# Two late blocks of a causal convolution computed on VectorE in fp32 single taps, with weight copies of their own and new tables of ranks

## The chip, the cores and the metric

The kernel runs on one core of one Trainium2 chip. The metric is the device time of one execution in microseconds (us). TensorE (PE) does the matmuls, VectorE (DVE) and ScalarE (ACT) move and combine data, GpSimd (POOL) issues the loads of x and of the weights, and SyncE (SP) issues the transfers to and from DRAM that go through its queue. All of them work on the same 16 DMA engines.

## The reference

The input x is 8 batches of 3200 positions by 256 channels. A filter is applied along the positions in the frequency domain, and the result goes through a gated linear unit whose gate comes from a causal convolution with 5 taps per channel:

```python
def _attn_ref(x, filt_r, filt_i):
    X = np.fft.rfft(x, axis=1)
    F = (filt_r + 1j * filt_i)[None, :, :]
    y = np.fft.irfft(X * F, n=x.shape[1], axis=1)
    return y.astype(np.float32)

def _moe_ref(x, w_val, conv_w, w_out):
    B, S, D = x.shape
    K = conv_w.shape[0]                       # 5
    xp = np.concatenate([np.zeros((B, K - 1, D)), x], axis=1)
    gate_pre = np.zeros((B, S, D))
    for k in range(K):
        gate_pre += conv_w[k][None, None, :] * xp[:, k:k + S, :]
    gate = 1.0 / (1.0 + np.exp(-gate_pre))
    return (gate * (x @ w_val) @ w_out).astype(np.float32)

# reference: _moe_ref(_attn_ref(x, filt_r, filt_i), ...)
```

## The kernel before

**Stages of a batch.** The transform of length 3200 is split into 100 by 32. For each batch, in order:

- `load_x`: eight loads of x (200 KB each, cast to bf16), issued by POOL into ten buffers `xt`.
- `s1` (matmuls on L467): eight steps of two matmuls, the transform of length 100; `so` evicts each from PSUM into the tile so.
- `turn` (L486): four transposes on VectorE that bring the 32 residues onto partitions.
- `s2` (L496): seven groups, the transform of length 32; `xs` evicts, and `zed` (L512) multiplies with the filter on VectorE: the spectral product z.
- `inva` (L527): seven groups, the first half of the inverse (the inverse-A product); `ue` evicts into the tile u, of which there is one buffer.
- `wr` writes u to a DRAM scratch (escr) and `lv` reads it back in another layout (vt, one buffer), both on SP's queue. Only batch 0 turns u on VectorE instead (`back`, L568).
- `ib` (L578): eight steps, the second half of the inverse; `ye` (L587, ScalarE) evicts them into yt, which has four zero columns (`halo`, a memset on POOL) ahead of its 3200 positions.

Then come the gate and the value, in seven blocks of positions, six of 512 and one of 128 (a quarter block):

- `conv` (L609): 20 matmuls with 64 by 64 diagonal matrices dg_t, two halves of the channels by five taps, four of them in the array's four quarters at a time. Its output lies with the channels in an order of its own.
- `gate` (L619, ScalarE): the sigmoid, from PSUM into gt.
- `val` (L628): four matmuls with wv_t, whose columns are permuted as the convolution's channels are.
- `gv` (L643, VectorE): the product of val in PSUM and gt.
- `outp` (L651): eight matmuls of gv with wo_t, permuted likewise; `oe` evicts, and `store` writes to DRAM from one of five buffers o.

**Who does what.** The evictions so, xs, ue and oe can go to either ScalarE (L458) or VectorE (L460); the products, transposes and gv are VectorE's alone, the gates and ye ScalarE's alone. PSUM is four slots of two banks; each of the matmul steps takes one slot until its eviction frees it.

**What sets the order.** `Plan` lists every step with a cost for each engine that can do it, what it depends on and which buffers it takes and gives back. It walks through time, and on each free engine puts the ready step of the lowest rank. The rank of a step is eight times the batch number plus `LAG[stage]`, plus `FIRST[stage]` for batch 0, plus `STEP[stage]` times the step's number. `STAY` is added for a change of the TensorE mode (row-tiled steps s2, inva, conv against the others), `LEAN` for an eviction on VectorE. The list that comes out is the fixed order of instructions on every engine. An engine executes its list in order, so an instruction that waits holds back all that stand behind it on that engine.

**The weights.** POOL waits until the filter has arrived (`gate_loads`), issues ten loads of x, then the eight weight DMAs of `load_w`, then further loads of x as buffers come free.

Of the kernel before, what the change touches and what calls it, by code (L numbers as in the profile page):

```python
# [20 lines left out]
NV = 4 * NS  # L21
TURN = (0,)

LAG = dict(lx=-36, s1=-112.5, so=-60, t=188, pd=-44.5, s2=33.5, xs=111.5, z=-11, ia=44.5,
           ue=37.5, k=-47, ib=73, ye=38.5, cv=84, ga=-76.5, vl=75, gv=-70.5, op=82, oe=29)
FIRST = dict(lx=-69, s1=32.5, so=44.5, t=56.5, pd=-52, s2=8, xs=4.5, z=-13, ia=-16.5, ue=49.5,
             k=-34, ib=-10.5, ye=10.5, cv=10.5, vl=-27.5, gv=3, op=99.5, oe=-45.5)
CONV = 1.0
STEP = dict(lx=0.25, s1=0.8, so=1.4, t=0.8, s2=1.25, xs=0.4, z=2.35, ue=0.5, k=1.35, ib=0.15,
            ye=1.8, cv=0.1, ga=2.1, vl=0, gv=0.4, op=0.2, oe=0.2)  # L30
STAY, LEAN = 17.5, 12
RC = 4
NCH = R // RC
UCH = [(m, min(2, NM - m)) for m in range(0, NM, 2)]
BLK = 512
NB = 7
MAGIC = 12582912.0
SEM = dict(PE=0.2, ACT=0.13, DVE=0.13, none=0.0)


class Plan:
# [9 lines left out]
    def add(self, name, engines, rank, deps, emit, take=(), give=(), land=0.0, mode=None,  # L51
            ps=0, free=()):
        self.tasks[name] = dict(engines=engines, rank=rank, deps=deps, emit=emit, take=take,
                                give=give, land=land, mode=mode, ps=ps, free=free, slots=[])

    def places(self, n):
        if n == 0:
# [7 lines left out]
    def run(self):  # L65
        left = dict(self.tasks)
        users, need = {}, {}
        for n, t in left.items():
            need[n] = len(t["deps"])
            for d in t["deps"]:  # L70
                users.setdefault(d, []).append(n)
        ready_at = {n: 0.0 for n in left}
        free = {}
        mode = turn = None
        gives = []
        ready = {n for n in left if need[n] == 0}
        order = []
        now = 0.0
        while left:
            gives.sort(key=lambda v: v[0])  # L80
            while gives and gives[0][0] <= now + 1e-9:
                for pool in gives.pop(0)[1]:
                    if isinstance(pool, int):
                        self.slots.append(pool)
                    else:
                        self.room[pool] += 1
            best = None
            for n in ready:
                t = left[n]
                if ready_at[n] > now + 1e-9:  # L90
                    continue
                if self.places(t["ps"]) is None or any(self.room[p] < 1 for p in t["take"]):
                    continue
                for e, cost in t["engines"].items():
                    if free.get(e, 0.0) <= now + 1e-9:
                        away = e == "PE" and t["mode"] != mode
                        other = e == "DVE" and len(t["engines"]) > 1
                        key = (t["rank"] + (self.stay if away else 0.0)
                               + (self.lean if other else 0.0), cost)
                        if e == "DQ":  # L100
                            key = (ready_at[n] + (1e4 if t["mode"] == turn else 0.0), 0.0)
# [36 lines left out]
        return order  # L138
# [3 lines left out]
def kernel(  # L142
# [37 lines left out]
    dg_t = cpool.tile([128, 2, K, 64], BF16, name="dg_t")  # L180
    wv_t = cpool.tile([128, 2, D], BF16, name="wv_t")
    wo_t = cpool.tile([128, 2, D], BF16, name="wo_t")

    dpool = ctx.enter_context(tc.tile_pool(name="scr", bufs=2, space=bass.MemoryType.DRAM))
    pp = ctx.enter_context(tc.tile_pool(name="ps", bufs=1, space=bass.MemoryType.PSUM))
    ps_all = pp.tile([128, 4, 1024], FP32, name="ps")
    NXT = 10
    xpool = ctx.enter_context(tc.tile_pool(name="xin", bufs=NXT))
    sopool = ctx.enter_context(tc.tile_pool(name="s1o", bufs=1))
    tpool = ctx.enter_context(tc.tile_pool(name="s2i", bufs=1))  # L190
# [81 lines left out]
    def load_w():  # L272
        for dh in range(2):
            for r in range(2):
                ch = 128 * dh + 64 * r
                nc.gpsimd.dma_start(
                    out=wv_t[:, dh, :].rearrange("p (r h j) -> p h r j", r=2, h=2)[:, r],
                    in_=moe_w_val[128 * dh:128 * dh + 128, 128 * r:128 * r + 128]
                    .rearrange("p (h j) -> p h j", h=2))
                nc.gpsimd.dma_start(out=wo_t[64 * dh:64 * dh + 64, r, :],  # L280
                                    in_=moe_w_out[ch:ch + 64, :])

    def sp_setup():
        cw = g["cw"] = g1.tile([128, 2, K], FP32, name="cw")
# [9 lines left out]
                                      in_=f_t[p:p + 32, w, :, m0:m1, :])  # L294

    def cf_dve():
        idx = g1.tile([128, 2, 2, 32], FP32, name="idx")
        V.scalar_tensor_tensor(idx[...], g["k1f"][...], g["pcol"][:, 0:1], g["phf"][...],
                               op0=ALU.mult, op1=ALU.add)
        ts(idx[...], idx[...], 0.01, ALU.mult)  # L300
# [146 lines left out]
        hold = g1.tile([128, 1], BF16, name="hold")  # L447
        nc.gpsimd.tensor_copy(hold[...], f_t[:, 1, 1, NM - 1, 0:1])

    NGB, NOB = 3, 5  # L450
    vpool = ctx.enter_context(tc.tile_pool(name="ivi", bufs=1))
    ypool = ctx.enter_context(tc.tile_pool(name="yout", bufs=2))
    gpool = ctx.enter_context(tc.tile_pool(name="gate", bufs=NGB))
    opool = ctx.enter_context(tc.tile_pool(name="ost", bufs=NOB))

    def copy(e, dst, src, **kw):
# [145 lines left out]
    def conv(b, c):  # L602
# [9 lines left out]
                                 start=(k == 0), stop=(k == K - 1))  # L612
        st["cv", b, c] = ps

    def gate(b, c):
        ps = st.pop(("cv", b, c))
        g = gpool.tile([128, 2, BLK], BF16, name="gt")
        w = width(c)
        nc.scalar.activation(g[:, :, 0:w], two_banks(ps, w), AF.Sigmoid)  # L619
        st["G", b, c] = g  # L620

    def val(b, c):
# [3 lines left out]
        for eh in range(2):  # L626
            for dh in range(2):
                nc.tensor.matmul(ps[:, 512 * eh:512 * eh + w],  # L628
                                 lhsT=wv_t[:, dh, 128 * eh:128 * eh + 128],
                                 rhs=y[:, dh, H + BLK * c:H + BLK * c + w],  # L630
                                 start=(dh == 0), stop=(dh == 1))
        st["vl", b, c] = ps
# [13 lines left out]
    def outp(b, c):  # L646
        gv_ = st.pop(("GV", b, c))
        ps = psum()
        for a in range(width(c) // 128):
            for eh in range(2):  # L650
                nc.tensor.matmul(ps[:, D * a:D * a + D],  # L651
                                 lhsT=gv_[:, eh, 128 * a:128 * a + 128], rhs=wo_t[:, eh, :],
                                 start=(eh == 0), stop=(eh == 1))
        st["op", b, c] = ps

# [7 lines left out]
    def store(b, c):  # L663
# [4 lines left out]
            in_=o[:, 0:w // 128 * D])  # L668


    plan = Plan(dict(xt=NXT, so=1, t=1, xs=3, z=3, u=1, e=2, v=1, y=2, g=NGB, gv=NGB, o=NOB), 4,
                stay=STAY, lean=LEAN)
    add = plan.add

# [7 lines left out]
    for b in range(B):  # L682
# [65 lines left out]
        add(f"ha{b}", {"POOL": 0.2}, at("ib"), [f"ye{b},0"], lambda e, b=b: halo(b))  # L748
        for c in range(NB):
            f = width(c) / BLK  # L750
            add(f"cv{b},{c}", {"PE": 1.08 * f}, at("cv", c),
                [f"ye{b},{j}" for j in range(NCH)] + [f"ha{b}", "dg0", "dg1"],
                lambda e, b=b, c=c: conv(b, c), ps=1, take=("g",), mode=1)
            add(f"ga{b},{c}", {"ACT": 0.77 * f + 0.16}, at("ga", c), [f"cv{b},{c}"],
                lambda e, b=b, c=c: gate(b, c), free=[f"cv{b},{c}"])
            add(f"vl{b},{c}", {"PE": 0.87 * f}, at("vl", c),
                [f"cv{b},{c}"] + ([f"vl{b},{c - 1}"] if c else []), lambda e, b=b, c=c: val(b, c),
                ps=1, take=("gv",), give=("y",) if c == NB - 1 else (), mode=0)
# [78 lines left out]
```

## Time and profile before

| | |
|---|---|
| time, median of 3 runs | 308.13 us (307.31 to 309.5) |
| the profiled execution | 308.17 us, of which 306.3 us are its span |
| mean granted TensorE clock | 0.975 of full speed |
| busy, share of the span: TensorE | 263.4 us (86%) |
| VectorE | 255.6 us (83%) |
| ScalarE | 254.3 us (83%) |
| GpSimd | 58.0 us (19%) |
| DMA: SP's queue, share of 16 engines | 50.4%, 51.79 MB |
| DMA: GpSimd's queue | 30.6%, 15.08 MB |
| chain that ended last, by engine | TensorE 41%, VectorE 20%, DMA 14%, ScalarE 12% |

The profile is one execution. Its span runs from the first to the last recorded instruction; the rest of the execution's time lies around it. A busy TensorE is not TensorE at its peak, because matmuls are pipelined. The idle time of an engine matters where that engine is the one that the others wait for, so the shares have to be read by stretches of the span, not as an average over it.

### The profile page before, as it was taken

The numbers are of one execution on the slowest core, as the hardware profiler recorded it, in microseconds if no ns is written. First come the engines' busy times: TensorE is split into PE (matmuls) and PEld (weight loads), VectorE is DVE, ScalarE is ACT, GpSimd is POOL, SyncE is SP. The second block draws the span as 40 slices with busy tenths as digits, with TensorE's granted clock in tenths as the row PEclk, the third lists the DMA queues.
The fourth block names the chain that finished last, engine by engine and source line by source line (L and its number), as shares of the span: only waits on it lengthen the run. The fifth ranks groups of instructions, "written<-read, shape, count | busy, mean of one in ns | idle before, by whom it ended". The sixth has DMA issues, their size and how long they took to land.

```text
span 306.3 us, 8876 instructions
## 1 busy us (share of the span) xinstructions
PE 263.4 (86%) x3658; PEld 160.3 (52%) x3684; DVE 255.6 (83%) x284; ACT 254.3 (83%) x301; POOL 58.0 (19%) x120
## 2 busy tenths in 40 slices
PE   2831789889988898999699999998999999999993
PEld 0120526345446446754467447836577676566562
DVE  7688997889999899998399999989999985455442
ACT  3864879999799899997689999999889977786663
POOL 8584467520140050032000210000000000000000
PEclk9999955999999999999999999999999999999998
DMA  6999599998899989999599898858355993947255
GB/s 91 185 161 164 95 183 122 187 189 219 282 218 274 344 161 246 299 268 230 156 286 324 263 218 269 317 204 280 121 190 210 327 333 108 327 162 277 89 208 223
DMA packets 53208, 67.44 MB, mean 220 GB/s; under 512 B 7792, under 2 KB 34032, under 8 KB 53168
## 3 DMA queue, kind: packets, MB, share of 16 engines
q1 hardware_dynamic: 41264, 51.79, 50.4%
q0 software_dynamic: 11904, 15.08, 30.6%
q8 instruction: 29, 0.48, 0.6%
q14 instruction: 11, 0.09, 0.1%
HBM read 42.08 MB, written 38.14 MB: 262 GB/s over the span
## 4 chain that ended last, share of the span: by engine, by line
PE 41%; DVE 20%; DMA 14%; ACT 12%; issue 6%; POOL 4%; SPq 0%; DVEq 0%; ACTq 0%; POOLq 0%
PE ps L609 12%; PE ps L651 10%; PE ps L628 9%; DVE xs L460 6%; DVE z L512 6%; DMA xt<-in_x_dram 5%; PE ps L578 4%; DVE gv L643 4%; DMA escr<-u 4%; ACT yt L587 3%; PE ps L527 3%; ACT so L458 3%; DVE u L460 3%; DMA f_t<-in_filt_r_dram 2%; PE ps L467 2%
## 5 line engine op out<-in xcount | busy, mean ns | idle before, releaser
L643 DVE TENSOR_TENSOR gv<-ps,gt 128x1024 bf16<-128x1024 f32 (+1 forms) x56 | 60.7, 1100 | 24.4 <-PE ps L628 17.5
L512 DVE TENSOR_TENSOR z<-xs,f_t 128x2048 bf16<-128x2048 bf16 (+1 forms) x56 | 62.1, 1140 | 1.5 <-DMA f_t<-in_filt_i_dram 0.9
L609 PE MATMUL ps<-yt,dg_t 64*64 64x512 bf16 (+1 forms) x1120 | 60.7, 354 | 0.6 <-ACT yt L587 0.5
L458 ACT ACTIVATE so<-ps 128x1024 bf16<-128x1024 f32 x55 | 53.7, 1044 | 7.9 <-PE ps L467 5.6
L619 ACT ACTIVATE gt<-ps 128x1024 bf16<-128x1024 f32 (+1 forms) x56 | 52.0, 944 | 7.7 <-PE ps L609 5.4
L587 ACT ACTIVATE yt<-ps 128x800 bf16<-128x800 f32 x64 | 51.4, 852 | 7.0 <-PE ps L578 6.8
L467 PE MATMUL ps<-xt,cf_t 100*128 100x512 bf16 x128 | 45.5, 443 | 11.2 <-DMA xt<-in_x_dram 7.1
L202 POOL DMA_DIRECT2D xt<-in_x_dram x64 | 35.4, 557 | 100.5 <-PE ps L467 96.5
L651 PE MATMUL ps<-wo_t,gv 128*128 128x256 bf16 x400 | 51.8, 272 | 0.6 <-DVE gv L643 0.6
L628 PE MATMUL ps<-yt,wv_t 128*128 128x512 bf16 (+1 forms) x198 | 50.5, 354 | 1.8 <-DVE xs L460 0.3
L458 ACT ACTIVATE o<-ps 128x1024 f32<-128x1024 f32 (+1 forms) x41 | 38.9, 957 | 10.0 <-PE ps L651 9.2
L609 PEld LDWEIGHTS <-dg_t 64*64 64x64 bf16 x1120 | 31.1, 106 | 21.8 <-issue 3.0
L651 PEld LDWEIGHTS <-gv 128*128 128x128 bf16 x400 | 37.0, 97 | 8.7 <-DVE gv L643 1.3
L458 ACT ACTIVATE u<-ps 128x1024 bf16<-128x1024 f32 (+1 forms) x35 | 35.4, 1022 | 7.2 <-PE ps L527 5.4
L486 DVE STREAM_TRANSPOSE tt<-so 128x1024 f32<-128x1024 f32 x32 | 38.4, 1225 | 2.6 <-ACT so L458 2.6
L527 PE MATMUL ps<-z,a_t 64*64 64x256 bf16 x416 | 28.3, 288 | 13.1 <-DVE z L512 9.0
L578 PEld LDWEIGHTS <-vt 104*128 104x128 bf16 (+1 forms) x512 | 30.1, 102 | 9.1 <-issue 2.4
L578 PE MATMUL ps<-ci_t,vt 104*128 104x100 f16 (+1 forms) x512 | 33.9, 214 | 0.7 <-DVE gv L643 0.4
L496 PE MATMUL ps<-tt,w_t 64*64 64x256 bf16 x416 | 23.2, 291 | 9.7 <-DVE tt L486 5.6
L460 DVE CAST xs<-ps 128x1024 bf16<-128x1024 f32 (+1 forms) x27 | 30.7, 1156 | 0.5 <-PE ps L496 0.4
L458 ACT ACTIVATE xs<-ps 128x1024 bf16<-128x1024 f32 (+1 forms) x29 | 27.2, 974 | 4.1 <-PE ps L496 4.1
L628 PEld LDWEIGHTS <-wv_t 128*128 128x128 bf16 x224 | 18.7, 97 | 19.8 <-issue 5.6
(94 smaller groups left out, 192.3 us busy)
## 6 DMA issues: line engine op xcount, KB each, us to landing
out_dram<-o SPq DMA_DIRECT2D x48, 512.0 KB
xt<-in_x_dram POOLq DMA_DIRECT2D x64, 200.0 KB, 7.2
escr<-u SPq DMA_DIRECT2D x42, 256.0 KB
vt<-escr SPq DMA_DIRECT2D x56, 192.0 KB
out_dram<-o SPq DMA_DIRECT2D x8, 128.0 KB
f_t<-f_t SPq DMA_DIRECT2D x4, 224.0 KB
escr<-u SPq DMA_DIRECT2D x7, 128.0 KB
vt<-escr SPq DMA_DIRECT2D x56, 16.0 KB
```

Source lines behind the costliest of these rows:

```text
L458: nc.scalar.activation(dst, src, AF.Copy, **kw)
L460: nc.vector.tensor_copy(dst, src)
L467: nc.tensor.matmul(ps[:, 512 * h:512 * h + 512], lhsT=cf_t[0:L].rearrange("p h c i -> p (h c i)"), rhs=xv[:, DQ // 2 * h:DQ // 2 * h + DQ ...
L486: nc.vector.transpose(dst, src)
L512: nc.vector.tensor_tensor(z[:, :, :, 0:nm * D], st.pop(("XS", b, u))[:, :, 0:nm * D].unsqueeze(1) .to_broadcast((128, 2, 2, nm * D)), f_t[ ...
L578: nc.tensor.matmul(ps[:, o:o + L], lhsT=v[rows, RC * j + a, 128 * dh:128 * dh + 128], rhs=ci_t[rows, way, :], start=True, stop=True)
L587: nc.scalar.activation(y[:, :, H:H + N].rearrange("p h (a r) -> p h a r", r=R)[:, :, :, RC * j:RC * j + RC], ps[:, :].rearrange("p (h n) - ...
L609: nc.tensor.matmul(ps[64 * dh:64 * dh + 64, 512 * r:512 * r + w], lhsT=dg_t[rows, dh, k, :], rhs=y[rows, dh, BLK * c + k:BLK * c + k + w], ...
L619: nc.scalar.activation(g[:, :, 0:w], two_banks(ps, w), AF.Sigmoid)
L628: nc.tensor.matmul(ps[:, 512 * eh:512 * eh + w], lhsT=wv_t[:, dh, 128 * eh:128 * eh + 128], rhs=y[:, dh, H + BLK * c:H + BLK * c + w], sta ...
L643: nc.vector.tensor_tensor(o, i0, i1, op=ALU.mult)
L651: nc.tensor.matmul(ps[:, D * a:D * a + D], lhsT=gv_[:, eh, 128 * a:128 * a + 128], rhs=wo_t[:, eh, :], start=(eh == 0), stop=(eh == 1))
```

## The change

The convolution of block 5 of batch 6 and of block 3 of batch 7 no longer runs on TensorE. `side` computes it on VectorE: for each of the two channel halves a tensor_scalar with tap 0 and four scalar_tensor_tensor with taps 1 to 4, each of 128 partitions by 512 elements, from yt (bf16) into a tile acc (fp32, one buffer), ten instructions per block. The sigmoid of such a block reads acc from SBUF in place of PSUM. Since acc has the channels in their natural order, val and outp of these blocks use unpermuted copies of the weights, wvs_t and wos_t, loaded by two more DMAs at the end of `load_w`.

There are nine buffers xt for ten and four buffers o for five, and the table's index tile idx shares the memory of phf. All values of LAG, FIRST, STEP, STAY and LEAN are new, so the order of the instructions changes on every engine, and with it the engine of many evictions. Ranks are compared after rounding, and ties go by the order in which the steps were added.

```diff
-LAG = dict(lx=-36, s1=-112.5, so=-60, t=188, pd=-44.5, s2=33.5, xs=111.5, z=-11, ia=44.5,
-           ue=37.5, k=-47, ib=73, ye=38.5, cv=84, ga=-76.5, vl=75, gv=-70.5, op=82, oe=29)
...
+LAG = dict(lx=-102, s1=-149.5, so=-28, t=-14.5, pd=22, s2=-148, xs=31, z=101.5, ia=35.5,
+           ue=174.5, k=-68.5, ib=48.5, ye=-127, cv=77, ga=-150, vl=-28, gv=-180, op=58, oe=-187)
...
-STAY, LEAN = 17.5, 12
+STAY, LEAN = 47.5, 70.5
...
+SIDE = [(6, 5), (7, 3)]
+SIDERANK = 0
...
-                        key = (t["rank"] + (self.stay if away else 0.0)
-                               + (self.lean if other else 0.0), cost)
+                        key = (round(t["rank"] + (self.stay if away else 0.0)
+                                     + (self.lean if other else 0.0), 6), cost, t["at"])
...
+    wvs_t = cpool.tile([128, 2, D], BF16, name="wvs_t")
+    wos_t = cpool.tile([128, 2, D], BF16, name="wos_t")
...
-    NXT = 10
+    NXT = 9
...
+        nc.gpsimd.dma_start(out=wvs_t[...], in_=moe_w_val.rearrange("(h p) e -> p h e", h=2))
+        nc.gpsimd.dma_start(out=wos_t[...], in_=moe_w_out.rearrange("(h p) e -> p h e", h=2))
...
-        idx = g1.tile([128, 2, 2, 32], FP32, name="idx")
+        idx = g["phf"]
...
-    NGB, NOB = 3, 5
+    NGB, NOB = 3, 4
...
+    apool = ctx.enter_context(tc.tile_pool(name="acc", bufs=1))
...
+    def side(b, c, n):
+
+        k, dh = n // 2, n % 2
+        if n == 0:
+            st["A", b, c] = apool.tile([128, 2, BLK], FP32, name="acc")
+        w = width(c)
+        acc = st["A", b, c][:, dh, 0:w]
+        src = st["Y", b][:, dh, BLK * c + k:BLK * c + k + w]
+        cw = g["cw"][:, dh, k:k + 1]
+        if k == 0:
+            nc.vector.tensor_scalar(acc, src, cw, None, op0=ALU.mult)
+        else:
+            nc.vector.scalar_tensor_tensor(acc, src, cw, acc, op0=ALU.mult, op1=ALU.add)
+
     def gate(b, c):
-        ps = st.pop(("cv", b, c))
+        ps = st.pop(("cv", b, c), None)
...
-        nc.scalar.activation(g[:, :, 0:w], two_banks(ps, w), AF.Sigmoid)
+        src = st.pop(("A", b, c))[:, :, 0:w] if ps is None else two_banks(ps, w)
+        nc.scalar.activation(g[:, :, 0:w], src, AF.Sigmoid)
...
-                                 lhsT=wv_t[:, dh, 128 * eh:128 * eh + 128],
+                                 lhsT=(wvs_t if (b, c) in SIDE else wv_t)[:, dh, 128 * eh:128 * eh + 128],
...
-                                 lhsT=gv_[:, eh, 128 * a:128 * a + 128], rhs=wo_t[:, eh, :],
+                                 lhsT=gv_[:, eh, 128 * a:128 * a + 128],
+                                 rhs=(wos_t if (b, c) in SIDE else wo_t)[:, eh, :],
...
+            if (b, c) in SIDE:
+                for n in range(2 * K):
+                    add(f"cx{b},{c},{n}", {"DVE": (0.28 if n < 2 else 0.54) * f + 0.07}, at("cv", c) + SIDERANK,
+                        [f"cx{b},{c},{n - 1}"] if n else
+                        [f"ye{b},{j}" for j in range(NCH)] + [f"ha{b}"],
+                        lambda e, b=b, c=c, n=n: side(b, c, n), take=() if n else ("g", "acc"))
...
-    add("wts", {"POOL": 5.0}, 8.5, ["hold"], lambda e: load_w())
+    add("wts", {"POOL": 6.2}, 8.5, ["hold"], lambda e: load_w())
...
-    for n, when in (("fl0", 25.0), ("fl1", 30.0)):
+    for n, when in (("fl0", 27.0), ("fl1", 31.0)):
```

More of the change, by code (lines that the diff above doesn't have):

```diff
@@ L22 @@
 TURN = (0,)
-LAG = dict(lx=-36, s1=-112.5, so=-60, t=188, pd=-44.5, s2=33.5, xs=111.5, z=-11, ia=44.5,
-           ue=37.5, k=-47, ib=73, ye=38.5, cv=84, ga=-76.5, vl=75, gv=-70.5, op=82, oe=29)
-FIRST = dict(lx=-69, s1=32.5, so=44.5, t=56.5, pd=-52, s2=8, xs=4.5, z=-13, ia=-16.5, ue=49.5,
-             k=-34, ib=-10.5, ye=10.5, cv=10.5, vl=-27.5, gv=3, op=99.5, oe=-45.5)
+LAG = dict(lx=-102, s1=-149.5, so=-28, t=-14.5, pd=22, s2=-148, xs=31, z=101.5, ia=35.5,
+           ue=174.5, k=-68.5, ib=48.5, ye=-127, cv=77, ga=-150, vl=-28, gv=-180, op=58, oe=-187)
+FIRST = dict(lx=-78, s1=53, so=101, t=149, pd=39.5, s2=17.5, xs=-62, z=-135, ia=6.5, ue=-57.5,
+             k=-35.5, ib=31.5, ye=61, cv=34.5, ga=-71, vl=33.5, gv=-7, op=65, oe=171)
 CONV = 1.0
-STEP = dict(lx=0.25, s1=0.8, so=1.4, t=0.8, s2=1.25, xs=0.4, z=2.35, ue=0.5, k=1.35, ib=0.15,
-            ye=1.8, cv=0.1, ga=2.1, vl=0, gv=0.4, op=0.2, oe=0.2)
-STAY, LEAN = 17.5, 12
+STEP = dict(lx=0, s1=0.45, so=0.25, pd=1.7, s2=1.75, xs=0.2, z=0.65, ia=1.2, ue=1.45, k=2.25,
+            ib=0.35, ye=0.4, cv=0.15, ga=0.5, vl=1.6, gv=1.7, op=1.65, oe=0.55)
+STAY, LEAN = 47.5, 70.5
 RC = 4
@@ L53, in add @@
         self.tasks[name] = dict(engines=engines, rank=rank, deps=deps, emit=emit, take=take,
-                                give=give, land=land, mode=mode, ps=ps, free=free, slots=[])
+                                give=give, land=land, mode=mode, ps=ps, free=free, slots=[],
+                                at=len(self.tasks))
     def places(self, n):
@@ L97, in run @@
                         other = e == "DVE" and len(t["engines"]) > 1
-                        key = (t["rank"] + (self.stay if away else 0.0)
-                               + (self.lean if other else 0.0), cost)
+                        key = (round(t["rank"] + (self.stay if away else 0.0)
+                                     + (self.lean if other else 0.0), 6), cost, t["at"])
                         if e == "DQ":
-                            key = (ready_at[n] + (1e4 if t["mode"] == turn else 0.0), 0.0)
+                            key = (round(ready_at[n] + (1e4 if t["mode"] == turn else 0.0), 6), 0.0,
+                                   t["at"])
                         if best is None or key < best[0]:
@@ L668, in store @@
             in_=o[:, 0:w // 128 * D])
-    plan = Plan(dict(xt=NXT, so=1, t=1, xs=3, z=3, u=1, e=2, v=1, y=2, g=NGB, gv=NGB, o=NOB), 4,
+    plan = Plan(dict(xt=NXT, so=1, t=1, xs=3, z=3, u=1, e=2, v=1, y=2, acc=1, g=NGB, gv=NGB, o=NOB), 4,
                 stay=STAY, lean=LEAN)
@@ L750 @@
             f = width(c) / BLK
[L751 to L755, printed above, removed]
+            if (b, c) in SIDE:
[4 more added lines that the diff above has]
+                        lambda e, b=b, c=c, n=n: side(b, c, n), take=() if n else ("g", "acc"))
+                add(f"cv{b},{c}", {"none": 0.0}, 0, [f"cx{b},{c},{2 * K - 1}"], None)
+                add(f"ga{b},{c}", {"ACT": 0.77 * f + 0.16}, at("ga", c), [f"cv{b},{c}"],
+                    lambda e, b=b, c=c: gate(b, c), give=("acc",))
+            else:
+                add(f"cv{b},{c}", {"PE": 1.08 * f}, at("cv", c),
+                    [f"ye{b},{j}" for j in range(NCH)] + [f"ha{b}", "dg0", "dg1"],
+                    lambda e, b=b, c=c: conv(b, c), ps=1, take=("g",), mode=1)
+                add(f"ga{b},{c}", {"ACT": 0.77 * f + 0.16}, at("ga", c), [f"cv{b},{c}"],
+                    lambda e, b=b, c=c: gate(b, c), free=[f"cv{b},{c}"])
             add(f"vl{b},{c}", {"PE": 0.87 * f}, at("vl", c),
```

## The prediction

> **What bounds the kernel now.** The page's second part was read first: the busy tenths of 40 slices, 7.66 us each.
>
> ```profile
> PE   2831789889988898999699999998999999999993
> ...
> DVE  7688997889999899998399999989999985455442
> ACT  3864879999799899997689999999889977786663
> ...
> PEclk9999955999999999999999999999999999999998
> ```
>
> Three phases show: a start in which nothing is full, a middle in which VectorE and ScalarE are at 9 but for one hole near slice 19, and from slice 33 on a tail where only TensorE is. The end of batch 7's last spectral product (L512, 244.7 us) divides middle from tail. Busy time of each engine (us, count), granted clock, DMA share and GB/s in both stretches:
>
> ```profile
> core 0: us, PE busy (x) PEld busy (x) DVE busy (x) ACT busy (x) POOL busy (x), PEclk, DMA share, GB/s
> 244.70:303.40 58.70, 55.77 (x718) 36.34 (x723) 31.36 (x31) 41.70 (x48) 0.10 (x1) 1.00 0.60 219
> 75.20:244.70 169.50, 157.87 (x2353) 99.29 (x2362) 160.10 (x152) 154.79 (x180) 17.23 (x36) 1.00 0.85 249
> ```
>
> In the middle VectorE idles 169.5 - 160.1 = 9.4 us; in the tail it idles 27.3 us while TensorE idles 2.9. So VectorE's amount of work sets when the middle ends, and TensorE's remaining work sets the rest. The hole, in the chain (start, us, what) and in the list of waits:
>
> ```profile
> 139.88 0.70 DVE u L460
> 140.60 10.74 DMA escr<-u
> 151.65 1.24 DVE u L460
> ```
>
> ```profile
> DVE u L460 <- DMA out_dram<-o: 5.0, 1, 5.0
> ```
>
> Batch 3's last piece of u landed in DRAM only 10.74 us after its issue, behind six stores; u is one buffer, so batch 4's first eviction of u waited, 5.0 us of it bare on VectorE.
>
> Prices come from the groups kept apart by shape (busy, mean ns) and from the timeline (start, us):
>
> ```profile
> L609 PE MATMUL ps<-yt,dg_t 64*64 64x512 bf16 x960 | 57.7, 377 | 0.6 <-ACT yt L587 0.5
> ...
> L512 DVE TENSOR_TENSOR z<-xs,f_t 128x2048 bf16<-128x2048 bf16 x48 | 56.8, 1217 | 1.5 <-DMA f_t<-in_filt_i_dram 0.9 <-ACT xs L458 0.4
> ...
> L345 DVE TENSOR_TENSOR vt<-e,e 128x1664 f32<-128x1664 f32 x1 | 1.9, 1892 | 0.0
> L219 DVE TENSOR_SCALAR ix<-ix 128x200 f32<-128x200 f32 x1 | 1.9, 1891 | 0.0
> ...
> L224 DVE TENSOR_TENSOR fyx<-ix,fyx 128x200 f32<-128x200 f32 x1 | 0.4, 368 | 0.0
> ...
> L223 DVE TENSOR_SCALAR fyx<-ix 128x200 f32<-128x200 f32 x1 | 0.3, 264 | 0.0
> ```
>
> ```profile
> 238.96 3.48 DVE L512 TENSOR_TENSOR z<-xs,f_t 128x2048 bf16<-128x2048 bf16 x3
> ```
>
> Three products in a row take 3.48 us though one alone takes 1.217: each further one costs 1.13, so 0.09 of an instruction overlaps with its neighbour. In full stretches every VectorE instruction of full size (product, gv, transpose, eviction) starts 1.13 to 1.15 after the last: taken as 1.135, half size 0.60, quarter 0.33. On TensorE the chain gives 3.25 us for three convolution blocks (L609 x60), 1.083 each, 0.86 for four matmuls of val (L628 x4), 0.88 for eight of outp (L651 x8); an ib step (L578) follows val by 0.36.
>
> **The change, part by part.** The whole order moves, since every table of ranks is new; so I count each kernel's instruction order between the same marks.
>
> *Middle, VectorE.* From the end of batch 1's last product (74.3) to that of batch 7's, the old order has 131 full, 14 half and 6 quarter instructions: 148.7 + 8.4 + 2.0 = 159.1 us, against 160.1 busy. The new one has 141, 8 and 10: 160.0 + 4.8 + 3.3 = 168.1. So **+9.0**: 18 evictions of so go from ScalarE to VectorE (9 before, 27 after) against 10 of xs and 4 of u that come off, and four more gv come before the mark. ScalarE becomes lighter and stays hidden.
>
> *Before the middle.* Two transposes of batch 2 move ahead of batch 1's last product: **+2.3**. Between ends 0 (VectorE idles about 4.9 us in this stretch) and 2.3 I take the full price, as the gaps there are under 1 us each.
>
> *Weight copies and one x buffer fewer.* POOL issues nine x loads instead of ten ahead of the weights, and ten weight DMAs instead of eight. Eight took from 42.18 to 50.38, 1.03 each. Batch 2's second x load, issued at 40.41 before, now follows them: 40.4 + 10 x 1.03 = 50.7, landing (median 7.2) at 57.9, where its first-stage matmul (L467) ran at 54.6. Behind that matmul wait batch 1's second-stage matmuls in TensorE's order. Bounds 0 (landing as fast as the weights' 4.9, slack eaten) to 4; I take **+1.5**, nearer the hidden end since VectorE has four transposes queued at that time.
>
> *The hole.* In the new order 11 full instructions stand on VectorE, and 9.9 us on TensorE, between a batch's last eviction of u and the next batch's first, in each of batches 2 to 4, against some 6 us at the hole. Landings of the last pieces otherwise took 1.8 to 5.8 us by the trace's landing events. I let the hole close: **-5.0**, with 0 as the other bound.
>
> *Tail, TensorE.* After the mark the old order has 15 full convolutions, 16 val, 18 outp, 16 ib, three quarter blocks of each kind and a last half product: 16.2 + 13.8 + 15.8 + 5.8 + 2.1 + 0.2 = 54.0, and ran 244.7 to 301.4, so 2.7 more for mode changes and two short waits. The new one has 11, 14, 14, 12: 11.9 + 12.1 + 12.3 + 4.4 + 2.1 + 0.2 = 43.0, with the same 2.7. **-11.0**: 2.2 of it are the two blocks taken from TensorE, the rest is work that now runs ahead of the mark.
>
> *The taps.* From 1892 ns at 1664 elements and 368 at 200, a two-input fp32 instruction costs 1.041 ns an element: 693 ns at 512. A tensor_scalar has 1125 (L348, 1664) and 264: 447 at 512. Sixteen and four make 12.9; overlapped by 0.09 each, 11.1; I take 12.0. VectorE's tail is then 18 full, one half, 6 quarter and the taps: 20.4 + 0.6 + 2.0 + 12.0 = 35.0 in 45.7 us. Each gv queued behind three to five taps (0.6 to 3.5 us) keeps outp waiting only if VectorE is late: before batch 7's first gv VectorE has some 25 us of work after the mark, TensorE some 31 before it needs it. So nothing on the path, with 0 to 2 as bounds. The gates from the accumulator cost ScalarE what others do.
>
> The row L219 ix shows a price beyond these: a tensor_scalar of 200 elements took 1891 ns where its like (L223) took 264, while POOL's memset of u ran from 26.08 for 1.40 us. The Trainium skill (SBUF — State Buffer, Who interferes with whom) says that a one-source VectorE instruction in a two-port mode and a GpSimd instruction exclude each other for their whole length. By it the first taps would cost 447 ns unless POOL works then. Without any rule: four at 1891 add 5.8 us to a tail with 10 to spare; POOL is busy 0.10 us in it, so I keep 447.
>
> Four stores in flight rather than five: landings after 165 us took 1.9 to 5.2 us, four outputs 3.5 or more: 0, at most 1.
>
> *Sum* against the profiled execution, 308.17 us (span 306.3; the median of the runs is 308.13): +9.0 + 2.3 + 1.5 - 5.0 - 11.0 = -3.2, so **305.0**, at the edge of what counts as faster (1%, about what a measurement of this kernel can tell from no change: below 305.05).
>
> **The rivals.**
> *The round trip through DRAM becomes the wait* (slower). TensorE's work between a batch's last inverse-A product and its first ib is 14.2 to 23.2 us in batches 4 to 7 before; in the new order it is 13.8, then 9.5, 10.4 and 9.8 in batches 5, 6, 7. An eviction (about 1.5 us), a landing in escr, one of vt's first piece and two issues (0.5 each) make 6.8 with the shortest landings of batches 4 to 7 (1.9 and 2.4). It decides from 9.5. With the landings that the trace has from 93 to 115 us (5.8 and 5.4) it is 13.7, which stops TensorE for 4.2, 3.3 and 3.9; with the first of them taken up by TensorE's slack, 7.2 more: 312. For it: ib is in TensorE's order, nothing passes it. Against: TensorE has some 10 us of slack in the middle, batch 7 alone is bare. Chance 0.21.
> *The hole stays*: 310.0. For it: DMA share 0.9 to 1.07 from 80 to 150 us. Chance 0.13.
> *The regular order loses nothing*: the other 4.4 us of idle in the middle shrink by half and the x loads and transposes hide (-2.2 - 1.5 - 2.3): 299. Chance 0.13.
> *Half clock in the tail*. The granted clock was 0.50 from 38.4 to 52.0, after a slice with TensorE at 1. One such stretch of 13.6 us in the tail costs 6.8: 311.8. It needs a bare wait of several us there; the longest so far is 0.3. Chance 0.03. The Trainium skill (TensorE: Matmul & The Clock Gate, HAM oscillation) puts the point at idle gaps of about 3.4 us; the trace's clock does not contradict it.
> *Taps dear*: all twenty at 1.89 make the tail 60.8 us of VectorE, 320; decides from 1.1 a tap. Chance 0.02.
>
> **How the numbers follow.** The forecast has 0.48, its own range 301 to 308 by the bounds above; it lies on the line, and as its two open costs (+2.3, +1.5) are at the high end or can only shrink, I give 0.31 of it to below 305.05. Faster: 0.31 + 0.13 = 0.44. Same: 0.17 + 0.13 = 0.30. Slower: 0.21 + 0.03 + 0.02 = 0.26. From 299 to 312 leaves out the outer half of the fast and of the round-trip case and both small ones: 2 in 10.
>
> **What would show it.** Right: batch 7's last product ends near 252.5, TensorE then runs 45 to 46 us without waits over 0.5, VectorE waits for no DMA over 1 us, taps take 0.6 to 0.7, first-stage matmuls of batch 2 wait for x near 55. Wrong: ib or vt among the waits for DMA in batches 5 to 7; the mark beyond 256; the middle's VectorE work off 168 by over 3; gv in the tail waiting behind taps with TensorE idle.

## The result and the profile after

The changed kernel takes 306.52 us (median of 20 runs, 303.46 to 309.63) against 308.35 us for the kernel before (20 runs, 305.43 to 311.04). The ratio is 0.9941, 95% interval 0.9916 to 0.9966: shorter by about 1.8 us or 0.6%, less than the 1% at which the prediction drew its line for faster. Its profiled execution took 305.65 us with a span of 303.9, against 308.17 and 306.3 before.

The busy tenths in 40 slices, here of 7.6 us each, from the page of the changed kernel (slices are counted from 0):

```profile
PE   2831759799997899999999999999999998999992
...
DVE  7788897689999999999999999999999997896952
ACT  3963879798798988898889988998999997787772
PEclk9999995689999999999999999999999999999998
```

The hole near slice 19 has gone: VectorE stands at 9 from slice 9 to slice 32, and behind that the taps fill what was a tail of fours and fives. The two stretches again (time, then busy time and count of each engine, the granted clock, DMA share and GB/s), now divided by the end of batch 1's last spectral product (78.1), that of batch 7's (252.4), called the mark from here on, and the end of TensorE's last outp (298.7):

```profile
core 0: us, PE busy (x) PEld busy (x) DVE busy (x) ACT busy (x) POOL busy (x), PEclk, DMA share, GB/s
78.10:252.40 174.30, 165.78 (x2465) 104.73 (x2482) 169.02 (x161) 157.08 (x181) 17.84 (x37) 1.00 0.86 251
252.40:298.70 46.30, 45.00 (x573) 28.80 (x570) 36.07 (x45) 34.88 (x41) 0.10 (x1) 1.00 0.61 222
```

Between the same events the kernel before had 74.3, 244.8 and 301.4. So the time went like this:

| stretch | before | after | difference | predicted |
|---|---|---|---|---|
| start to batch 1's last product | 74.3 | 78.1 | +3.8 | +2.3 + 1.5 = +3.8 |
| from there to batch 7's last product | 170.5 | 174.3 | +3.8 | +9.0 - 5.0 = +4.0 |
| from there to the end of TensorE's last outp | 56.6 | 46.2 | -10.4 | -11.0 |

The three stretches together are 2.8 us shorter, the span is 2.4 shorter: behind the last outp the changed kernel takes 5.2 us, the one before 4.9. The predicted mark was 244.7 + 3.8 + 4.0 = 252.5, the measured one is 252.4. In the middle VectorE's busy time rose from 161.1 to 169.0 (+7.9) and its idle time fell from 9.4 to 5.3 us (-4.1): both terms were taken about 1 us too large, and they have opposite signs. TensorE's busy time in the same stretch rose by 6.9 us (158.9 to 165.8) and ScalarE's by 1.3 (155.8 to 157.1). In VectorE's timeline (start, length, instruction, in brackets the idle time before it and what ended it) one batch of the middle looks like the next; these are all of the waits from 160 to 200 us, as a copy of o and a gv once per batch:

```profile
160.25 1.22 DVE L469 COPY o<-ps 128x1024 f32<-128x1024 f32 x1 [0.73 <-ACT yt L596]
172.24 1.22 DVE L667 TENSOR_TENSOR gv<-ps,gt 128x1024 bf16<-128x1024 f32 x1 [0.43 <-issue]
192.34 1.23 DVE L469 COPY o<-ps 128x1024 f32<-128x1024 f32 x1 [0.72 <-ACT yt L596]
```

The period is 192.34 - 160.25 = 32.1 us with 1.2 us of VectorE waits in it. None of them is for a DMA.

The tail of VectorE, in the same view:

```profile
256.99 1.55 DVE L667 TENSOR_TENSOR gv<-ps,gt 128x1024 bf16<-128x1024 f32 x2 [1.60 <-ACT gt L643]
...
261.22 0.87 DVE L634 TENSOR_SCALAR acc<-yt,cw 128x512 f32<-128x512 bf16 x2
262.01 2.07 DVE L636 SCALAR_TENSOR_TENSOR acc<-yt,cw,acc 128x512 f32<-128x512 bf16 x3
264.11 2.44 DVE L667 TENSOR_TENSOR gv<-ps,gt 128x1024 bf16<-128x1024 f32 x2
```

Two first taps take 0.87 us and three further ones 2.07, and the gv behind them starts without a bracket, which means without idle. The tile acc's own durations (minimum, median and maximum in ns, first and last start):

```profile
L636 DVE SCALAR_TENSOR_TENSOR acc<-yt,cw,acc x16: 739/744/746, 262.0 to 288.5; 128x512 f32<-128x512 bf16 x16
L634 DVE TENSOR_SCALAR acc<-yt,cw x4: 476/478/480, 261.2 to 280.6; 128x512 f32<-128x512 bf16 x4
```

One tap alone is 744 ns; from start to start it is 0.66 us (262.01 to 264.11 is three and a gap), a first tap 478 ns and 0.40. So the twenty take 16 x 0.66 + 4 x 0.40 = 12.2 us, against 12.0 in the prediction.

The list of waits (total, times, longest) on transfers, of the changed kernel:

```profile
PE ps L476 <- DMA xt<-in_x_dram: 10.3, 7, 5.6
...
PEld L587 <- DMA vt<-escr: 3.2, 5, 0.9
...
PE ps L587 <- DMA vt<-escr: 1.6, 3, 0.8
```

The first belongs to the x loads (7.1 in the kernel before): batch 2's second first-stage step started at 55.8, where it was 54.7. The other two are the round trip through DRAM, the rival with the highest chance. They are there, but 0.9 us at the longest, where the rival needed 3.3 to 4.2 per batch.

### The profile page after: what moved, and what is told of

Same layout as the page of the kernel before. It is cut to its first block, busy times and chain, and to the rows that moved or that the text cites. A ratio compares the mean times of both kernels' runs of the same rounds, so it can differ in the third digit from the quotient of the medians.

```text
span 303.9 us, 8836 instructions
## 1 busy us (share of the span) xinstructions
PE 262.5 (86%) x3612; PEld 160.4 (53%) x3644; DVE 271.1 (89%) x309; ACT 251.7 (83%) x296; POOL 59.6 (20%) x122
## 4 chain that ended last, share of the span: by engine, by line
PE 48%; DMA 20%; DVE 10%; ACT 7%; issue 5%; POOL 5%; SPq 2%; DVEq 0%; POOLq 0%; ACTq 0%
PE ps L618 14%; PE ps L652 11%; PE ps L675 11%; DMA vt<-escr 7%; DMA xt<-in_x_dram 5%; PE ps L587 4%; PE ps L476 4%; DMA f_t<-in_filt_i_dram 4%; ACT yt L596 3%; PE ps L536 3%; DVE gv L667 3%; POOL xt L208 3%; ACT o L467 2%; DVE tt L495 2%; DMA f_t<-in_filt_r_dram 2%
## 5 line engine op out<-in xcount | busy, mean ns | idle before, releaser
L618 PE MATMUL ps<-yt,dg_t 64*64 64x512 bf16 (+1 forms) x1080 | 59.8, 358 | 0.1
L643 ACT ACTIVATE gt<-ps 128x1024 bf16<-128x1024 f32 (+1 forms) x54 | 49.6, 936 | 5.5 <-PE ps L618 4.3
L652 PE MATMUL ps<-yt,wv_t 128*128 128x512 bf16 (+1 forms) x184 | 48.7, 352 | 2.6 <-ACT gt L643 0.5
L675 PE MATMUL ps<-wo_t,gv 128*128 128x256 bf16 x384 | 49.5, 272 | 0.4 <-DVE gv L667 0.3
L467 ACT ACTIVATE o<-ps 128x1024 f32<-128x1024 f32 x40 | 40.9, 1024 | 10.1 <-PE ps L675 8.6
L467 ACT ACTIVATE so<-ps 128x1024 bf16<-128x1024 f32 x37 | 37.2, 1025 | 11.8 <-PE ps L476 11.3
L467 ACT ACTIVATE u<-ps 128x1024 bf16<-128x1024 f32 (+1 forms) x39 | 37.5, 975 | 5.0 <-PE ps L536 4.7
L467 ACT ACTIVATE xs<-ps 128x1024 bf16<-128x1024 f32 (+1 forms) x39 | 35.5, 948 | 5.0 <-PE ps L505 4.8
L469 DVE CAST so<-ps 128x1024 bf16<-128x1024 f32 x27 | 32.0, 1215 | 4.2 <-PE ps L476 4.0
L652 PEld LDWEIGHTS <-wv_t 128*128 128x128 bf16 x216 | 17.7, 97 | 22.3 <-issue 7.9
```

The source lines that it names most:

```text
L467: nc.scalar.activation(dst, src, AF.Copy, **kw)
L618: nc.tensor.matmul(ps[64 * dh:64 * dh + 64, 512 * r:512 * r + w], lhsT=dg_t[rows, dh, k, :], rhs=y[rows, dh, BLK * c + k:BLK * c + k + w], ...
L643: nc.scalar.activation(g[:, :, 0:w], src, AF.Sigmoid)
L652: nc.tensor.matmul(ps[:, 512 * eh:512 * eh + w], lhsT=(wvs_t if (b, c) in SIDE else wv_t)[:, dh, 128 * eh:128 * eh + 128], rhs=y[:, dh, H ...
L675: nc.tensor.matmul(ps[:, D * a:D * a + D], lhsT=gv_[:, eh, 128 * a:128 * a + 128], rhs=(wos_t if (b, c) in SIDE else wo_t)[:, eh, :], star ...
```

## The experiments

The ratio of each is to the kernel before, from the runs of its own chip. To compare with the changed kernel the ratio is divided by 0.9941, and what it differs from 1 is multiplied by 308 us; the intervals of both together leave 1.2 to 2 us either way. Stretches of the span are read from one profile of each kernel.

### The tail is TensorE's: no taps

```diff
-SIDE = [(6, 5), (7, 3)]
+SIDE = []
```

> The changed kernel with no block on the taps: all blocks of the convolution on TensorE again; new tables, nine x buffers, four output buffers and the weight copies stay. Theory (the tail is TensorE's work): two blocks at 1.083 come back to TensorE behind the mark, so 2.2 us longer than the changed kernel (ratio to before 0.994 + 0.007 = 1.001), the mark at 252.4 as in the changed kernel within 0.5. Rival (the taps hold up gv in the tail): no slower than the changed kernel, by up to 1.6 us (the longest wait of the changed kernel's tail) faster.

Ratio 0.9992 (0.996 to 1.0023): 1.6 us longer than the changed kernel. In the profiles the mark is at 253.2, 0.8 later than in the changed kernel where at most 0.5 was expected, in a run whose start was already 1.1 us later (batch 1's last product at 79.2). TensorE's last outp ends at 301.7: 48.5 us behind the mark against 46.2, so 2.3 us for two blocks that were counted at 2.2. VectorE's timeline where the taps had been:

```profile
264.83 2.46 DVE L667 TENSOR_TENSOR gv<-ps,gt 128x1024 bf16<-128x1024 f32 x2 [2.79 <-ACT gt L643]
...
271.78 2.43 DVE L667 TENSOR_TENSOR gv<-ps,gt 128x1024 bf16<-128x1024 f32 x2 [2.10 <-PE ps L652]
...
279.06 2.44 DVE L667 TENSOR_TENSOR gv<-ps,gt 128x1024 bf16<-128x1024 f32 x2 [2.44 <-PE ps L652]
```

Here gv waits for TensorE and ScalarE, 2 to 3 us each time; the taps lay in these waits. The rival, that they hold up gv, is out. The two blocks are worth 2.3 us of the tail; the other 8.1 of the 10.4 by which it shrank come from the order.

The new order without the taps is no faster than the kernel before, though: 0.9992. It still carries the weight copies and the missing buffers, which only the taps need.

### The order or the taps: the tables of before

The changed kernel with the LAG, FIRST, STEP, STAY and LEAN of the kernel before:

```diff
-STAY, LEAN = 47.5, 70.5
+STAY, LEAN = 17.5, 12
```

> The changed kernel with the rank tables of the kernel before: taps, weight copies, nine x buffers, four output buffers, but not the new order. Its order has 161.3 us of VectorE work between the marks (159.1 before, 168.1 changed). Theory (what the change gains comes from the order: the hole closed and TensorE's work taken out of the tail): the hole behind batch 3's last write of u stays (a wait of VectorE for escr of 3 us or more), 2.2 us more VectorE work and 2.0 for the copies against the two blocks (2.2) and at most 5.7 of TensorE work less in the tail, so 306.5 to 310 us, ratio 0.995 to 1.007. Rival (the taps are the gain): 306.5 or less, ratio 0.994 or less.

Ratio 1.013 (1.0077 to 1.0183), 4.0 us longer than the kernel before and 5.9 longer than the changed one. The theory's range ended at 1.007, so the old order costs even more than it said. The rival, that the taps alone are the gain, is out: with the old order they come with a loss. Nor is the new order alone a gain while the copies are loaded early, as the run without taps shows; the 1.8 us need both. The hole is there, in VectorE's waits:

```profile
DVE u L469 <- DMA escr<-u: 5.2, 1, 5.2
```

Batch 1's last product ends at 76.6 (74.3 before). This order has the copies and nine x buffers, but no early transposes, so this **+2.3** is the price of the copies and of the missing buffer, as far as one profile of each can tell. The middle takes 174.0 us (to 250.6) where it took 170.5, 3.5 more where the counted work of VectorE is 2.2 more, and the tail gives 2.5 back. That the middle grew by more than its work was not followed up.

### The weight copies: loaded later

```diff
-        nc.gpsimd.dma_start(out=wvs_t[...], in_=moe_w_val.rearrange("(h p) e -> p h e", h=2))
-        nc.gpsimd.dma_start(out=wos_t[...], in_=moe_w_out.rearrange("(h p) e -> p h e", h=2))
...
+        if (b, j) == (5, 0):
+            nc.gpsimd.dma_start(out=wvs_t[...], in_=moe_w_val.rearrange("(h p) e -> p h e", h=2))
+            nc.gpsimd.dma_start(out=wos_t[...], in_=moe_w_out.rearrange("(h p) e -> p h e", h=2))
```

> The changed kernel with the two weight copies loaded just before batch 5's first x load, not ahead of batch 2's x loads. Theory (x loads behind the copies delay batch 2's first stage, term of 1.5 us): batch 2's first-stage matmuls start up to 2 us earlier, batch 1's last product ends near 76.6 instead of 78.1, and the whole is 1.5 us shorter (ratio 0.989). Rival (VectorE had other work then, the 3.8 us by which batch 1's last product is late is all transposes): the product stays at 78.1 and the time within 0.5 us.

Ratio 0.9876 (0.9836 to 0.9916), 304.61 us: 2.0 us shorter than the changed kernel (0.6 to 3.4). Batch 2's second first-stage step starts at 54.9 for 55.8, the eighth at 63.4 for 65.5. TensorE in the changed kernel and here:

```profile
55.82 1.03 PE L476 MATMUL ps<-xt,cf_t 100*128 100x512 bf16 x2 [1.29 <-DMA xt<-in_x_dram]
```

```profile
54.89 0.60 PE L477 MATMUL ps<-xt,cf_t 100*128 100x512 bf16 x2
```

TensorE stands bare for x in batch 2's first stage in all eight kernels of this document that load the copies ahead of these x loads, for 0.9 to 2.7 us, and in none of the four others. So the copies were on the path.

How much they cost is known less well. Batch 1's last product ends at 76.4 for 78.1, but this event moves by itself: in the seven profiles with the new order and early copies it ends between 76.9 and 79.2, though VectorE's list up to there is the same in all, and in the two with the old order and no copies (the kernel before and no_stores) at 74.3 and 73.3. So 1.7 us for the copies, and the 2.1 that are then left of the shift from 74.3 for the two transposes (2.3 in the sum), are good to a microsecond or so.

The copies cost about what the taps bring: 2.0 us by this run, against 1.6 by the run without taps and 2.3 in the tail. With early copies, then, the gain over the kernel before should be the order's, an estimate from these two runs; the new order with neither taps nor copies was not run.

Not all of the lead arrives. By the end of batch 3's last product it is 1.0 us instead of 1.7 (the whole span of the profile is 0.9 shorter), and the reason stands in TensorE's timeline and behind it in VectorE's:

```profile
123.85 0.51 PE L588 MATMUL ps<-ci_t,vt 104*128 104x100 f16 x8 [0.27 <-DMA vt<-escr]
125.72 0.51 PE L588 MATMUL ps<-ci_t,vt 104*128 104x100 f16 x8 [0.48 <-DMA vt<-escr]
```

```profile
127.20 1.23 DVE L470 COPY o<-ps 128x1024 f32<-128x1024 f32 x1 [1.79 <-ACT yt L597]
```

In the changed kernel no ib step waits there. The last pieces of batch 2's round trip don't come earlier by as much as TensorE does, so ib waits for them, ye for ib, and VectorE's copy of o waits 1.79 us where it waited 0.72. This is the rival's mechanism, in the next place where something is gained.

### The hole: fewer stores ahead of it

The kernel before, with two lines added in `store`:

```diff
+        if b == 1 and c < 6:
+            return
```

> The kernel before without the stores of the first six blocks of batch 1's output (that part of the output is not written; the rest is unchanged). Theory (batch 3's last write to escr waits for its turn behind stores, and VectorE stands bare for it): the wait of 5.0 us for the output's and escr's transfers goes and the whole is 5.0 shorter, 303 us, ratio 0.984. Rival (the hole only takes up slack that comes back later): within 1 us, ratio 0.997 to 1.003. Third: the landing stays at 10 us because other transfers hold it, and the time stays.

Ratio 0.9931 (0.99 to 0.9963): 2.1 us shorter, between theory and rival. The timeline of VectorE at the hole:

```profile
148.13 1.23 DVE L460 CAST u<-ps 128x1024 bf16<-128x1024 f32 x1 [2.48 <-DMA vt<-escr]
```

The wait was halved, from 5.0 to 2.5 us, and what it now ends on, by the profile, is the read back of vt. The middle went from 170.5 to 167.9 us (73.3 to 241.2): 2.6 shorter for a wait that is 2.5 shorter. So a microsecond of this hole is a microsecond of time, and leaving out the six stores took half of it, not all.

### Is VectorE the bound of the middle: one more instruction on each engine

Four kernels, each the changed one with one step of batches 3 to 6 made twice, the second time over the first.

```diff
+        for _ in range(2 if b in (3, 4, 5, 6) and u == 0 else 1):
+          nc.vector.tensor_tensor(
...
+        for a in [*range(nm)] * (2 if b in (3, 4, 5, 6) and u in (1, 3, 5) else 1):
...
+        for _ in range(2 if b in (3, 4, 5, 6) and c == 1 else 1):
+            nc.scalar.activation(g[:, :, 0:w], src, AF.Sigmoid)
```

The first is VectorE's, the second TensorE's, the third ScalarE's; the fourth kernel has `c == 4` in the third.

> The changed kernel with the first spectral product of batches 3, 4, 5 and 6 made twice (four more VectorE instructions of full size, 1.135 us each, nothing else). Theory (VectorE's amount of work sets when the middle ends): +4.5 us, the mark from 252.4 to 256.9. Rival (the middle is set by TensorE or by a loop through the buffers, with VectorE's 5.3 us of idle in it free): +1 us or less.

> The changed kernel with the matmuls of inverse A made twice for the second, fourth and sixth chunk of batches 3, 4, 5 and 6 (48 x 4 more matmuls, 0.43 us a chunk, 5.2 us of TensorE in all). Theory (VectorE sets the middle, TensorE has 8 us of idle there): +1.5 us or less. Rival (TensorE's order sets the middle): +4 to +5.2 us, with the mark later by as much.

> The changed kernel with one gate (the second block's sigmoid) of batches 3, 4, 5 and 6 made twice: four more full ScalarE instructions, 0.90 us each, 3.6 in all. Theory (VectorE sets the middle, ScalarE has 17 us of idle there): +1 us or less (ratio 0.994 to 0.9975). Rival (the three engines stand in one loop through few PSUM buffers, so that any of them delays it, as 5.2 us of TensorE cost 3.5): +2.4 us, two thirds of it.

> The changed kernel with the gate of the fifth block (not the second, as in extra_act) of batches 3 to 6 made twice: 0.90 us four times. Theory (three engines in one loop, a delay anywhere on ScalarE comes through): about +2.7 us again, ratio 1.003. Rival (only the places just ahead of an eviction that VectorE needs are dear; ScalarE's 17 us of idle cover the others): +0.7 us or less, ratio 0.9965 or less.

| added work | ratio to before, interval | longer than the changed kernel, us | of the work, ahead of the mark | middle, us (174.3) | tail, us (46.2) |
|---|---|---|---|---|---|
| VectorE, 4.5 us | 1.0109 (1.0067 to 1.015) | 5.2 | 4.5 | 179.0 (+4.7) | 46.2 |
| TensorE, 5.2 us | 1.0054 (1.0021 to 1.0087) | 3.5 | 5.2 | 178.1 (+3.8) | 46.2 |
| ScalarE, second block, 3.6 us | 1.003 (0.9993 to 1.0067) | 2.8 | 2.7 | 177.3 (+3.0) | 46.7 (+0.5) |
| ScalarE, fifth block, 3.6 us | 1.0012 (0.9972 to 1.0053) | 2.2 | 1.8 | 176.6 (+2.3) | 47.9 (+1.7) |

VectorE's work passes through whole, as the theory has it. But 73% of TensorE's comes through too (3.8 of 5.2), although it had 8.5 us of idle in the middle, and ScalarE's likewise with 17.2 of idle. Not all of ScalarE's doubled gates lie in the middle: three of the four of the second block and two of the four of the fifth come ahead of the mark (39 and 38 gates there for 36), the others in the tail. So the better sum for them runs from the end of batch 3's last product, ahead of which none is doubled, to TensorE's last outp: 160.1 us in the changed kernel, 163.0 in both of these, 2.9 us for 3.6 of work. The theory expected 1.5 us for TensorE and 1 for ScalarE: it falls in that part. For the fifth block the ratio's interval by itself doesn't exclude the rival's +0.7; the 2.9 us of the profile speak for the loop.

How it happens can be seen with the gate of the second block doubled. First ScalarE, then TensorE, then VectorE, in the timelines of that kernel:

```profile
170.64 3.15 ACT L644 ACTIVATE gt<-ps 128x1024 bf16<-128x1024 f32 x3
```

```profile
173.84 0.60 PE L476 MATMUL ps<-xt,cf_t 100*128 100x512 bf16 x2 [0.70 <-ACT gt L644]
```

```profile
172.67 1.22 DVE L668 TENSOR_TENSOR gv<-ps,gt 128x1024 bf16<-128x1024 f32 x1 [0.44 <-issue]
174.54 3.49 DVE L469 CAST so<-ps 128x1024 bf16<-128x1024 f32 x3 [0.64 <-PE ps L476]
```

The gates hold a PSUM slot about 1 us longer (three in 3.15 us, two in 2.10 in the changed kernel), the first-stage matmul that is to use the slot starts 0.70 us later, and VectorE, which has just finished gv and next has to evict that matmul, stands 0.64 us. The bracket of 0.64 is new; the one of 0.44 is not. So the idle time that ScalarE and TensorE show in the middle lies between steps of a chain through four PSUM slots, and for the work added here most of it was no reserve.

### A block on the taps in the middle

```diff
-SIDE = [(6, 5), (7, 3)]
+SIDE = [(3, 3), (6, 5), (7, 3)]
```

> The changed kernel with a third block on the taps, block 3 of batch 3, which stands in the middle where VectorE is full (the order is planned again with it). Its order has 170.7 us of VectorE work between the marks against 167.8 in the changed kernel by the same count, and 46.0 us of TensorE work behind the mark against 42.8. Theory (a block on VectorE pays only where VectorE has idle): +2.9 + 3.2 = 6.1 us, ratio 1.014. Rival (TensorE's work counts as much in the middle, so that a block taken from it pays there too): 1 us shorter to no change, ratio 0.991 to 0.994.

Ratio 1.0113 (1.0052 to 1.0173), 5.3 us longer than the changed kernel, against 6.1 expected: the theory's sum fits, and the rival is out. What one block costs by itself the run doesn't show, since its order was planned again: against the changed kernel the middle of its profile is 5.5 us longer (2.9 expected) and the tail 2.8 (3.2 expected).

The profiled execution was 8.4 us longer in its span (312.3), and part of that is the clock. The stretches around it:

```profile
188.00:190.00 2.00, 0.94 (x28) 0.54 (x21) 1.55 (x3) 0.33 (x1) 0.00 (x0) 1.00 0.04 8
190.00:192.00 2.00, 0.82 (x16) 0.46 (x16) 2.00 (x2) 2.00 (x3) 0.00 (x0) 0.82 0.72 256
192.00:194.00 2.00, 1.57 (x5) 0.68 (x6) 2.00 (x3) 1.47 (x2) 0.00 (x0) 0.50 0.90 259
194.00:196.00 2.00, 2.00 (x13) 0.97 (x11) 1.55 (x2) 0.84 (x1) 0.00 (x0) 0.50 0.77 247
196.00:198.00 2.00, 2.00 (x20) 0.83 (x19) 1.23 (x1) 0.51 (x1) 0.00 (x0) 0.50 0.83 242
```

```profile
190.75 0.82 PE L505 MATMUL ps<-tt,w_t 64*64 64x256 bf16 x16 [1.38 <-ACT u L467]
192.20 0.58 PE L652 MATMUL ps<-yt,wvs_t 128*128 128x512 bf16 x1 [0.64 <-DVE xs L469]
```

In each row the busy times of TensorE, its weight loads, VectorE and ScalarE follow the length; the granted clock is the third value from the end. In the 4 us ahead of the fall (187.3 to 191.3) TensorE was busy for 2.03. The clock was then 0.50 until about 198, some 7 us; at half clock that is 3.5 us of TensorE's work, an estimate. The other three executions have a mean granted clock of 0.977 to 0.994 against 0.959 here and take 309.70 to 311.43 us against 313.96, so this fall is shown for the profiled one only.

### Other tables with the late copies

The kernel with late copies, with all five tables changed once more and the taps on other blocks:

```diff
-STAY, LEAN = 47.5, 70.5
+STAY, LEAN = 45.6, 91.9
...
-SIDE = [(6, 5), (7, 3)]
+SIDE = [(6, 5), (7, 4)]
```

> The late weight copies together with other rank tables and the taps on blocks 5 of batch 6 and 4 of batch 7. By the sum of the prediction: 170.6 us of VectorE work between the marks against 167.8, the same tail (42.8 us of TensorE, 34.9 of VectorE), so 2.8 us longer than late_copies, ratio 0.997. Rival (the waits between the engines weigh as much as VectorE's count, and the tables were chosen for fewer of them): up to 1 us shorter than late_copies, ratio 0.984 to 0.988.

Ratio 0.9898 (0.9851 to 0.9945), 304.59 us: the same as with late copies alone (304.61), between the two expectations. In the profiles its middle takes 178.3 us (73.2 to 251.5) against 175.2 (76.4 to 251.6) with late copies alone, 3.1 longer where 2.8 was counted. But the stretch ahead of it is 3.1 shorter, with three instructions of VectorE fewer in it: work had only moved across the mark. My sum for this run looked at one side of it.

## Why the prediction was right, point by point

**The forecast** was 305.0 against a profiled execution of 308.17; the changed kernel's profiled execution took 305.65, its median 306.52. By the ratio the change is -1.8 us where the sum said -3.2. That lies well inside the range of 299 to 312, but on the no-change side of the line at 305.05, to which the prediction gave 0.30, and not on the faster side, which had 0.44.

**Middle, VectorE (+9.0)**: busy time +7.9. The count was too low by 2.0 us for the kernel before (159.1 against 161.1) and by 0.9 for the changed one (168.1 against 169.0). (The 160.1 that the prediction sets beside 159.1 starts at 75.2 and not at 74.3. Its 9 and 27 evictions of so are those of the whole kernel; in the middle they are 4 and 22, the same 18 more.) Work added to VectorE came through whole, so its work does set the end of the middle. It is not alone in that: TensorE's work there rose by 6.9 us, for which the sum has nothing, and work added to TensorE came through by 73%. How much of the middle's +3.8 is TensorE's wasn't separated.

**ScalarE "becomes lighter and stays hidden"**: the step is wrong. Over the whole kernel ScalarE's work went from 254.3 to 251.7 us, but in the middle it rose from 155.8 to 157.1. Nor is it hidden: of the 3.6 us added to it 2.9 came through in the profiles. That the sum didn't suffer more is luck, since the new order asked only 1.3 us more of ScalarE there. The slack of some 10 us that I gave TensorE in the middle as an argument against the round-trip rival fails likewise: most of it isn't slack.

**Transposes (+2.3) and weight copies (+1.5)**: together 3.8 measured, 3.8 predicted. That they agree to a tenth is luck: with the same instructions this event ended anywhere from 76.9 to 79.2. Apart, the copies were 1.7 by late_copies and 2.3 by old_tables_taps, more than the 1.5 taken but inside the bounds, and 2.1 is left for the transposes. The choice of the hidden end, because VectorE had four transposes queued, was the weaker one.

**The hole (-5.0)**: no wait of VectorE for a DMA remains, so the 5.0 are gone, but the rest of its idle time in the middle grew from 4.4 to 5.3 us, which leaves -4.1. The six stores were only half its cause, as the kernel without them shows. It is the new order that closed the hole, since with the old tables it is back at 5.2 us; that the distance between the two evictions of u does it is argued and not shown.

**Tail (-11.0)**: -10.4, 8.1 by the order and 2.3 by the two blocks. TensorE's waits there are 0.45 us at the longest, as forecast below 0.5.

**Taps (0 on the path, 12.0 us on VectorE)**: 12.2, and without them the tail is longer by just the two blocks. The prediction's own prices give 11.1, and it took 12.0 without a reason; a tap takes 744 ns where it had 693. **Four buffers o (0)**: no wait for a store shows in the tail.

**The rivals**: the hole didn't stay, taps weren't dear, the clock stayed at 1.00 in middle and tail, and VectorE's other idle in the middle did not shrink. The round trip shows as waits of up to 0.9 us, and with late copies it begins to take back what is won.

## What to carry to other kernels

Divide the span at the events where the limit changes, count each engine's instructions between them, and check that what leaves one stretch doesn't reappear in the next: three such sums put the mark within 0.1 us here, with luck, since two terms were off by about 1 us each and cancelled. Moving work to another engine pays where that engine waits (two blocks: 2.3 us in the tail) and did not pay where it is full (a third block in the middle, with the order that it brought: 5.3 us longer). Count with it what the move needs: the weight copies cost as much as the taps brought. Idle time of an engine inside a chain of few slots is not free time: add work to it and measure before counting on it. Two small loads ahead of the x loads in a queue held the first stage up; moving them behind took off 2.0 us and makes, with 0.9876 (0.9836 to 0.9916) of the kernel before, one of the two fastest versions here. The other, with tables of its own, can't be told from it.

## What the runs showed of the hardware

The granted clock of TensorE fell to 0.50 in mid run (mid_taps, about 191 to 198 us) without any wait of several us: the longest was 1.38 us, just ahead of the fall, and TensorE was busy for 51% of the 4 us before it. The kernel before has such a fall at its start: the clock was 1.00 from 35.0 us and fell at 38.4, TensorE was busy for 1.56 of these 3.4 us, and its longest wait since 30.5 was 1.39 us. My rival on the clock had asked for one bare wait of several us; in these two falls there was none within 7.8 us. The Trainium skill (TensorE: Matmul & The Clock Gate, A second HAM failure mode: psum-queue depth-cycling) tells of short idles between groups of matmuls that make the clock swing; these two traces agree, with 0.50 after busy shares of 51% and 46%.

A scalar_tensor_tensor of 128 x 512 with an fp32 accumulator takes 744 ns alone and 0.66 us from start to start, so neighbours on VectorE overlap by 0.08 us, about as long as for a full-size instruction (1.22 us alone, 1.135 from start to start).
